# Opening of a state-space kernel generator: first unit's phase and sines moved into the tables' stage

## The chip, the core and the metric

One core of one Trainium2 chip runs the whole program in one launch. The metric is the device time of the program in microseconds (us), the median of three timed runs. The profiles are of single executions of the same program, taken by the hardware profiler.

## What is computed

The reference runs four layers on a sequence of 2048 rows and 640 channels: a state-space convolution, an attention with one shared key and value head, and both again. Only the convolution kernel `K` matters for this change. It is the same for both convolution layers and is generated once, at the start of the program:

```python
dt = jnp.exp(log_dt)[:, None]
logdA = dt * (A_re + 1j * A_im)
P = jnp.exp(logdA[:, :, None] * l[None, None, :])        # 640 x 128 x 2048
K = jnp.einsum("dn,dnl,dn->dl", Cc, P, dt * Bc).real     # 640 x 2048
```

## The kernel before, in words

The program has five parts: the generator of `K` (`kgen`), a convolution, an attention, a convolution and an attention. The change touches the generator, which runs from the start of the program to about 300 us.

The generator has two stages. The first, `kg_tables` (from line 203), is here called **the tables' stage**. On tiles of 128 x 640 it works out four quantities per channel and state: the turn of one step (`thr`), of 32 steps (`th1`), the starting phase (`ph`) and the decay (`are`), with a logarithmic weight (`lw`). Each is split into three bf16 parts in a staging tile `hth1`, `hthr`, `hph`, `hlw`, `hare`. The parts then have to change their layout from channels on partitions to (part, channel) rows, in the three tables `tb` (from `th1`), `ta` (from `thr` and `ph`) and `tm` (from `are` and `lw`). `send` does that through DRAM for `th1`, `thr` and `are`: one copy out (`hd...`) and three back. `send_late` does it straight from the staging tile for `ph` and `lw`: three small copies (one per part, 16 partitions, 20 KB) for each of eight groups q of channels. The 48 small copies are here called **the late sends**; in the order of SyncE they stand as triples, `ta` of group 0, `tm` of group 0, `ta` of group 1, and so on to `tm` of group 7. A copy reads `hph` or `hlw` when it runs, so these two staging tiles are in use until the last late send has landed.

The second stage is the loop over 20 **units** u, each 32 channels by 128 states. A unit goes through these steps:

- `phase(u, h)`, h = 0 or 1: two matmuls (tile `ph`, one buffer in PSUM) give a phase, and VectorE takes its fraction with two instructions, `r` and `f` (128 x 1024).
- `trig(u, h)` on ScalarE: `fa` (absolute value), a sine and a cosine, into `C1`, `S1` for h = 0 and into `C2`, `S2` for h = 1.
- `sizes(u, k)`, k = 0, 1, 2: two matmuls each (tile `pe`, two buffers). k = 0, 1 read the 48 rows of `tm` from `are`; k = 2 reads also the rows from `lw`.
- `exps(u, k)` on ScalarE: exponentials into `M1` (k = 0, 1) and `M2` (k = 2).
- `products(u, k)`: two VectorE instructions each. k = 0 makes `e1r` from `M1` and `C1`, k = 1 multiplies `M1` by `S1`, k = 2 multiplies `C2` and `S2` by `M2`.
- `sums(u, ...)`: 64 small fp32 matmuls into `pk`; `store(u - 3)` copies `pk` to `kst` on ScalarE and, every fourth unit, to DRAM (`kd`).

Sine and exponential use different function tables on ScalarE, so a pair of units is done together: six exponentials, a table load, four `trig`, a table load. Group q of `ta` and `tm` is what unit u = q reads (modulo 8).

The order of PE, ScalarE and VectorE in the loop is written out by hand (`manual_schedule`); the order of SyncE's copies is manual only in the tables' stage, and elsewhere set by the scheduler. Products of unit u - 1, sums of unit u - 2 and phases of unit u + 1 are woven into turn u. `load_x` reads the residual stream `x` (eight copies of 640 KB), which the statistics (`stats`, one call in each of turns 5 to 12, the rest at the end) read.

Tiles come from pools, one region of memory each. All tiles of the tables' stage are in pool `kgq`, which is closed at its end; the loop's pool `kgb` is then opened where `kgq` was. A loop's tile that lies where a tile of the tables' stage lay waits until the earlier tile has been read for the last time.

Of the kernel before, what the change touches and what calls it, by code (L numbers as in the profile page):

```python
# [11 lines left out]
F32 = mybir.dt.float32  # L12
# [9 lines left out]
P = 128  # L22
# [134 lines left out]
class Net:  # L157
# [42 lines left out]
        with ExitStack() as ctx:  # L200
            self._kgen(ctx)

    def kg_tables(self, pp, hs, t3, SH, ldt, aim, are_raw, bre, bim, cre, cim, ta, tb, tm):

        nc = self.nc
        V, S, T, A = (nc.vector.tensor_tensor, nc.vector.scalar_tensor_tensor, nc.vector.tensor_scalar,
                      nc.scalar.activation)
        dt, th, are, thr, th1, ph = pp.tile([P, 5], F32, name="dt"), *(  # L210
            t3(n) for n in ("th", "are", "thr", "th1", "ph"))
        wr, wi, u0, u1, u2, u3, lw = (t3(n) for n in ("wr", "wi", "u0", "u1", "u2", "u3", "lw"))
        ar, ai, mx, mn, gt = (t3(n) for n in ("ar", "ai", "mx", "mn", "gt"))
        res = {n: t3("res" + n) for n in hs}

        def cast(n, src, k):
            A(hs[n][:, k], src if k == 0 else res[n], AF.Copy)

        def rest(n, src, k):
            V(res[n], src if k == 0 else res[n], hs[n][:, k], ALU.subtract)  # L220

        def send(n, dst, between=lambda: None):
            hd = self.dr.tile([P, 3, 5 * NST], BF16, name="hd" + n)
            nc.sync.dma_start(hd, hs[n].rearrange("p k t s -> p k (t s)"))
            between()
# [24 lines left out]
        rest("th1", th1, 0)  # L250
        cast("th1", th1, 1)
        V(mx, ar, ai, ALU.max)
        V(mn, ar, ai, ALU.min)
        T(mx, mx, 1e-37, None, ALU.max)
        rest("th1", th1, 1)
        cast("th1", th1, 2)
        send("th1", tb)
        cast("thr", thr, 0)
        nc.vector.reciprocal(u0, mx)
        V(u0, mn, u0, ALU.mult)  # L260
        for t in range(5):
            A(are[:, t], are_raw[:, t], AF.Copy, scale=dt[:, t : t + 1])
        cast("are", are, 0)

        A(u1, u0, AF.Arctan)
        V(gt, ai, ar, ALU.is_gt)
        rest("thr", thr, 0)
        cast("thr", thr, 1)
        T(wr, wr, 0.0, 0.5, ALU.is_lt, ALU.mult)
        S(u1, gt, 0.5 * math.pi, u1, op0=ALU.mult, op1=ALU.subtract)  # L270
        A(u1, u1, AF.Abs, scale=1.0 / TWO_PI)
        T(wi, wi, 0.0, -2.0, ALU.is_lt, ALU.mult)
        rest("thr", thr, 1)
        V(u1, wr, u1, ALU.subtract)
        A(u1, u1, AF.Abs)
        cast("thr", thr, 2)
        send("thr", ta)
        T(ph, th1, 32.0, None, ALU.mult)
        self.frac(pp, ph, ph, SH)
        S(u1, wi, 1.0, u1, op0=ALU.add, op1=ALU.mult)  # L280
        V(ph, ph, u1, ALU.add)
        self.frac(pp, ph, ph, SH)

        A(u2, u0, AF.Square)
        A(lw, mx, AF.Ln)
        A(u3, u2, AF.Ln, bias=1.0)
        nc.vector.tensor_copy(hs["ph"][:, 0], ph)
        rest("ph", ph, 0)
        nc.vector.tensor_copy(hs["ph"][:, 1], res["ph"])
        rest("ph", ph, 1)  # L290
        nc.vector.tensor_copy(hs["ph"][:, 2], res["ph"])
        rest("are", are, 0)
        cast("are", are, 1)
        S(lw, u3, 0.5, lw, op0=ALU.mult, op1=ALU.add)
        for t in range(5):
            T(lw[:, t], lw[:, t], ldt[:, t : t + 1], None, ALU.add)
        rest("are", are, 1)
        cast("are", are, 2)
        send("are", tm, lambda: send_late(0, ta, hs["ph"]))
        nc.vector.tensor_copy(hs["lw"][:, 0], lw)  # L300
        rest("lw", lw, 0)
        nc.vector.tensor_copy(hs["lw"][:, 1], res["lw"])
        rest("lw", lw, 1)
        nc.vector.tensor_copy(hs["lw"][:, 2], res["lw"])
        for q in range(8):
            if q > 0:
                send_late(q, ta, hs["ph"])
            send_late(q, tm, hs["lw"])

    def _kgen(self, ctx):  # L310
# [11 lines left out]
        with tc.tile_pool(name="kgq", bufs=1) as pp:  # L322
            SH = [P, 5, NST]

            def t3(name):
                return pp.tile(SH, F32, name=name)


            hs = {n: pp.tile([P, 3, 5, NST], BF16, name="h" + n)
                  for n in ("ph", "lw", "th1", "thr", "are")}  # L330
            ldt = pp.tile([P, 5], F32, name="ldt")
            nc.sync.dma_start(ldt, ins["A_log_dt"])
            raw = {}
            for n, eng in (("A_A_im", nc.sync), ("A_C_re", nc.scalar), ("A_B_re", nc.sync),
                           ("A_C_im", nc.scalar), ("A_B_im", nc.sync), ("A_A_re", nc.scalar)):
                raw[n] = t3("r" + n)
                eng.dma_start(raw[n], ins[n].rearrange("(t p) n -> p t n", p=P))
            nc.sync.dma_start(kg, ins["c_kg"])
            bre, bim, cre, cim = (raw["A_" + n] for n in ("B_re", "B_im", "C_re", "C_im"))
            with tc.manual_schedule(engines={mybir.EngineType.Activation, mybir.EngineType.DVE,  # L340
                                             mybir.EngineType.SP}):
                self.kg_tables(pp, hs, t3, SH, ldt, raw["A_A_im"], raw["A_A_re"], bre, bim, cre, cim,
                               ta, tb, tm)

        bp = ctx.enter_context(tc.tile_pool(name="kgb", bufs=2, reuse_waits="tile"))
# [5 lines left out]
        KST[0, 0] = bp.tile([P, 64, 32], F32, tag="kst", bufs=2, name="kst00")  # L351

        def big(tag, u, x, bufs=2):
            return bp.tile([P, 16, 2, x], F32, tag=tag, bufs=bufs, name=f"{tag}_{u}")

        def swap(a):
            return a.rearrange("p d a s -> p a d s")
# [16 lines left out]
        def phase(u, h):  # L374
            if (u, h) not in PH:
                phase_first(u, h)
            pp = PH.pop((u, h))
            r = bp.tile([P, 1024], BF16, tag="r", bufs=2, name=f"r{u}{h}")
            self.magic_round(r, pp)
            F[u, h] = bp.tile([P, 1024], F32, tag="f", bufs=4, name=f"f{u}{h}")  # L380
            nc.vector.tensor_tensor(F[u, h], pp, r, ALU.subtract)

        def trig(u, h):
# [9 lines left out]
            fa = bp.tile([P, 1024], F32, tag="fa", bufs=1, name=f"fa{u}{h}")  # L393
            nc.scalar.activation(fa, f, AF.Abs)
            nc.scalar.activation(s, f.rearrange("p (a d s) -> p a d s", a=2, d=16), AF.Sin, scale=TWO_PI)
            nc.scalar.activation(c, fa.rearrange("p (a d s) -> p a d s", a=2, d=16), AF.Sin,
                                 scale=-TWO_PI, bias=self.halfpi)

        def sizes(u, k):

            pe = PE_[u, k] = kp.tile([P, 1024], F32, tag="pe", bufs=2, name=f"pe{u}{k}")
# [60 lines left out]


        n = len(units)
        engines = {mybir.EngineType.PE, mybir.EngineType.Activation, mybir.EngineType.DVE}
        with tc.manual_schedule(engines=engines):
            for h in range(2):
                phase(0, h)
            for u in range(n + 3):
                now, nxt, prod, tot = u < n, u + 1 < n, 0 < u <= n, 2 <= u < n + 2  # L470
                odd = u % 2 == 1
                if u >= 3:
# [43 lines left out]
                        exps(u, 2)  # L516
                if tot:
                    sums(u - 2, range(7, 8))
                if u == 0:
                    self.load_x()  # L520
                    nc.sync.dma_start(self.ident, ins["c_id"])
                if 5 <= u < 13:
                    self.stats(u - 5)
# [836 lines left out]
```

## Time and profile before

| | |
|---|---|
| median of 3 runs | 3025.67 us (3024.11 to 3025.82) |
| the profiled execution | 3025.52 us, span in the profile 3023.7 us |
| busy, whole span | PE 93%, ScalarE (ACT) 80%, VectorE (DVE) 46%, GpSimd (POOL) 1% |
| tables' stage | 0 to about 43 us |
| opening of the loop (units 0 and 1) | about 43 to 72 us |
| loop over the other units | about 72 to 296 us |
| mean granted clock of TensorE | 0.958 |

Engines in the rows: PE and PEld (TensorE's matmuls and weight loads), DVE, ACT, POOL, and SPq and POOLq for the copies that SyncE and GpSimd issue. L with a number is the line of the kernel before. A timeline row gives start, duration, engine, line, operation, output<-input, sizes and count; in brackets stands the idle time of the engine just before the row, and what ended it. Rows of copies on SPq show the time of issuing, not of the transfer. Clock and DMA columns of a stretch are means over it.

### The profile page before, as it was taken

To read this page: it belongs to the slowest core of one execution; us is meant where nothing else is said; L and a number is where in the kernel's file an instruction comes from. 1 tells how busy PE (TensorE), PEld (TensorE's weight loads), DVE (VectorE), ACT (ScalarE), POOL (GpSimd) and SP (SyncE) were. 2 spreads that over 40 slices of the span, in tenths; PEclk is the share of its full clock that TensorE was granted. 3 is DMA by queue.
4 is the path that set the end of the run, shared out by engine and by line. 5 is a ranking of instruction groups with operands and counts; after the bars stand their busy time and mean duration, and the time that the engine had idled before them with its cause. 6 is when DMAs were issued, how large, how long until landed. Compare 5 with 4: busy or idle time off the path is not lost. (4 is left out here: it accounts for less than half of the span.)

```text
span 3023.7 us, 52365 instructions
## 1 busy us (share of the span) xinstructions
PE 2797.2 (93%) x21696; PEld 1284.0 (42%) x21696; DVE 1402.3 (46%) x1788; ACT 2427.3 (80%) x2910; POOL 45.1 (1%) x117
## 2 busy tenths in 40 slices
PE   2776989998999999999999899798999999999998
PEld 0333979775233323333232689673233333323333
DVE  7999899942123232322323499721222223222222
ACT  5888333444999999999999532438999999999997
POOL 0001000000000000000000000000000000000000
PEclk9855999999999999999999999899999999999999
DMA  6114531133200010000100211131100101110100
GB/s 145 33 22 112 186 143 56 46 115 111 80 22 25 22 27 21 26 25 22 25 22 20 113 56 42 58 131 56 27 24 23 43 22 26 39 28 21 43 19 23
DMA packets 109104, 158.82 MB, mean 53 GB/s; under 512 B 58948, under 2 KB 65092, under 8 KB 105236
## 3 DMA queue, kind: packets, MB, share of 16 engines
q1 hardware_dynamic: 102680, 137.70, 15.7%
q0 software_dynamic: 4208, 16.67, 1.5%
q8 instruction: 175, 2.87, 0.4%
q10 hardware_dynamic: 1968, 0.98, 0.1%
q14 instruction: 73, 0.60, 0.1%
HBM read 95.22 MB, written 48.04 MB: 47 GB/s over the span
## 5 line engine op out<-in xcount | busy, mean ns | idle before, releaser
L1158 ACT ACTIVATE pt<-scb 128x1024 f32<-128x1024 f32 x1024 | 942.2, 1116 | 7.5 <-DMA qpb<-mxd 4.5
L1158 ACT ACTIVATE pt<-scd 128x1024 f32<-128x1024 f32 x1024 | 942.2, 1117 | 7.0 <-PE scd L1154 5.4
L1168 PE MATMUL pod<-pt,vt 128*32 128x512 f32 x4096 | 547.1, 606 | 4.4 <-DVE on L1185 0.2
L1168 PE MATMUL pob<-pt,vt 128*32 128x512 f32 x4096 | 547.0, 606 | 4.4 <-DVE on L1185 0.3
L1154 PE MATMUL scb<-qpb,kt 62*128 62x512 f32 x2048 | 385.9, 451 | 6.2 <-DVEq L1103 5.8
L1154 PE MATMUL scd<-qpd,kt 62*128 62x512 f32 x2048 | 385.9, 451 | 5.6 <-PEq L1103 5.3
L1154 PEld LDWEIGHTS scb<-qpb,kt 62*128 62x128 f32 x2048 | 165.9, 185 | 402.1 <-ACT pt L1158 392.6
L1154 PEld LDWEIGHTS scd<-qpd,kt 62*128 62x128 f32 x2048 | 166.0, 185 | 401.7 <-ACT pt L1158 392.4
L1216 DVE TENSOR_TENSOR x<-pyd,x 128x320 f32<-128x320 f32 x146 | 71.8, 492 | 560.8 <-PE pyd L1228 560.8
L1216 DVE TENSOR_TENSOR x<-pyb,x 128x320 f32<-128x320 f32 x146 | 71.8, 492 | 547.6 <-PE pyb L1228 547.6
L1188 DVE RECIPROCAL rc<-rc 128x512 f32<-128x512 f32 x62 | 207.9, 3354 | 2.1
L1168 PEld LDWEIGHTS pob<-pt,vt 128*32 128x32 f32 x4096 | 80.6, 108 | 178.2 <-issue 160.2
L1168 PEld LDWEIGHTS pod<-pt,vt 128*32 128x32 f32 x4096 | 80.6, 108 | 178.0 <-issue 160.0
L601 PE MATMUL za<-xna,wf 128*128 128x256 f32 x512 | 113.0, 383 | 2.5 <-ACT xna L757 2.5
L601 PE MATMUL zc<-xnc,wf 128*128 128x256 f32 x512 | 111.5, 379 | 2.7 <-ACT xnc L757 2.7
L603 ACT ACTIVATE Aa<-za 128x1024 f32<-128x1024 f32 x16 | 16.4, 1023 | 118.5 <-PE za L601 117.3
L603 ACT ACTIVATE Ac<-zc 128x1024 f32<-128x1024 f32 x16 | 16.4, 1023 | 113.7 <-PE zc L601 113.7
L1228 PE MATMUL pyd<-wo,ot 128*32 128x320 f32 x1168 | 105.3, 432 | 0.0
L1228 PE MATMUL pyb<-wo,ot 128*32 128x320 f32 x1168 | 105.3, 432 | 0.0
L601 PEld LDWEIGHTS za<-xna,wf 128*128 128x128 f32 x512 | 97.8, 192 | 16.6 <-ACT xna L757 3.3
L601 PEld LDWEIGHTS zc<-xnc,wf 128*128 128x128 f32 x512 | 96.9, 190 | 16.3 <-ACT xnc L757 3.3
L800 PE MATMUL yc<-Ac,wi 128*128 128x128 f32 x640 | 78.4, 286 | 15.8 <-DVE Ac L114 13.1
(312 smaller groups left out, 3107.2 us busy)
## 6 DMA issues: line engine op xcount, KB each, us to landing
kh<-kh SPq DMA_DIRECT2D x10, 2048.0 KB
kh<-kn SPq DMA_DIRECT2D x5, 2048.0 KB
qhd<-qh SPq DMA_DIRECT2D x40, 256.0 KB
qld<-ql SPq DMA_DIRECT2D x40, 256.0 KB
qpb<-qhd SPq DMA_DIRECT2D x256, 40.0 KB
qpd<-qhd SPq DMA_DIRECT2D x256, 40.0 KB
ot<-on SPq DMA_DIRECT2D x216, 40.0 KB
wf<-in_c_wf POOLq DMA_DIRECT2D x16, 512.0 KB, 7.9
```

The source lines that it names most:

```text
L601: nc.tensor.matmul(zv[:, :, c, kk], self.wf[:, t + 4 * h, j, c, kk], x, start=(n == 0), stop=(n == 3))
L603: nc.scalar.activation(A.rearrange("p (o s) d -> p o s d", o=2)[:, :, 2 * t : 2 * t + 2], z.rearrange("p (c o e) -> p o c e", c=2, o=2), A ...
L800: nc.tensor.matmul(y[:, s * DC : (s + 1) * DC], self.wi[:, t, j, c_, kk], v[:, 2 * t + c_, kk], start=(i == 0 and not whole), stop=(i == 3 ...
L1154: nc.tensor.matmul(sc[:, 512 * par : 512 * par + 512], kt[rows, 128 * t : 128 * t + 128], qps[nb, hg, pr][rows], start=True, stop=True)
L1158: nc.scalar.activation(pt, sc, AF.Exp, scale=SCALE)
L1168: nc.tensor.matmul(po[32 * j : 32 * j + 32], vt[:, t], pts[step, j // 2][:, 512 * (j % 2) : 512 * (j % 2) + 512], start=(t == 0), stop=(t ...
L1188: nc.vector.reciprocal(rc, rc)
L1216: nc.vector.tensor_tensor(xh, py, xh, ALU.add)
L1228: nc.tensor.matmul(py[j : j + m], o[:, 128 * i + j : 128 * i + j + m], w[:, 320 * half : 320 * half + 320], start=start, stop=stop)
```

## The change

The change does these things:

- `phase(0, 0)` and `trig(0, 0)` of unit 0 are done inside the tables' stage (`begin()`), after the `ph` parts and before `lw` is finished.
- The splitting of `are` and its `send` come earlier, behind those of `thr`; the first triple of late sends (`ta`, group 0) follows it.
- Steps of units 0 and 1 are written out one by one: exponentials of both units first, then the sines `trig(0, 1)`, `trig(1, 0)`, `trig(1, 1)`. Turns from unit 2 on are as before.
- Most tiles of `phase` and `trig` and the `kst` tiles get a pool of their own (`kga`), opened before `kgq`, so that they don't lie where the tables' tiles lie.
- Twelve of the tables' fp32 tiles, the inputs' among them, are put into the memory of `x`. `x` is therefore loaded later: all eight copies stand behind the last late send, and wait for a small ScalarE instruction that writes `x`.
- In `kgq` the staging tiles come first, in the order `are`, `thr`, `th1`, a filler of 768 bytes, `ph`, `lw`.
- The order of SyncE's copies is manual in the loop too, and the load of `ident` stands in every turn from u = 2 to 21 (20 times 64 KB) in place of once.

```diff
-        res = {n: t3("res" + n) for n in hs}
+        res = {n: t3("res" + n) for n in ("ph", "lw", "th1", "thr", "are")}
...
         rest("thr", thr, 0)
         cast("thr", thr, 1)
+        rest("are", are, 0)
+        cast("are", are, 1)
...
         send("thr", ta)
+        rest("are", are, 1)
+        cast("are", are, 2)
+        send("are", tm)
...
         nc.vector.tensor_copy(hs["ph"][:, 2], res["ph"])
-        rest("are", are, 0)
-        cast("are", are, 1)
+        send_late(0, ta, hs["ph"])
+        begin()
         S(lw, u3, 0.5, lw, op0=ALU.mult, op1=ALU.add)
...
-        rest("are", are, 1)
-        cast("are", are, 2)
-        send("are", tm, lambda: send_late(0, ta, hs["ph"]))
...
+        ba = ctx.enter_context(tc.tile_pool(name="kga", bufs=2, reuse_waits="tile"))
...
+            pool = ba if tag in ("c1", "s1") else bp
+            return pool.tile([P, 16, 2, x], F32, tag=tag, bufs=bufs, name=f"{tag}_{u}")
...
+        def begin():
+            phase(0, 0)
+            trig(0, 0)
+
...
+            homes = [self.x.rearrange("p t d -> p (t d)")[:, 640 * k : 640 * k + 640].rearrange(
+                "p (t s) -> p t s", t=5) for k in range(12)]
+            homes += [pp.tile(SH, F32, name=f"t{k}") for k in range(16)]
+
             def t3(name):
-                return pp.tile(SH, F32, name=name)
-
-
-            hs = {n: pp.tile([P, 3, 5, NST], BF16, name="h" + n)
-                  for n in ("ph", "lw", "th1", "thr", "are")}
+                return homes.pop(0)
+
+            hs = {}
+            for n in ("are", "thr", "th1", "", "ph", "lw"):
+                if n:
+                    hs[n] = pp.tile([P, 3, 5, NST], BF16, name="h" + n)
+                else:
+                    pp.tile([P, 192], F32, name="space")
...
-            for h in range(2):
-                phase(0, h)
-            for u in range(n + 3):
+            phase(0, 1)
+            phase_first(1, 0)
+            for k in range(2):
+                sizes(0, k)
+                exps(0, k)
+            phase(1, 0)
+            sizes(0, 2)
+            exps(0, 2)
+            nc.scalar.activation(self.x[:, :, 0], M1[0][:, :, 0, 0], AF.Copy)
+            self.load_x()
+            products(0, 0)
+            for k in range(2):
+                sizes(1, k)
+                exps(1, k)
+            phase(1, 1)
+            sizes(1, 2)
+            exps(1, 2)
+            trig(0, 1)
+            phase(2, 0)
+            products(0, 1)
+            trig(1, 0)
+            phase(2, 1)
+            products(0, 2)
+            trig(1, 1)
+            for u in range(2, n + 3):
...
                 if tot:
                     sums(u - 2, range(7, 8))
-                if u == 0:
-                    self.load_x()
                     nc.sync.dma_start(self.ident, ins["c_id"])
```

How the change moves instructions, at the three places that count. In these rows no time is told; `hph`, `hlw`, `hare` are staging tiles, `m` is `M1` or `M2`, `c`, `s` are `C1`, `C2`, `S1`, `S2`, and a number in a name is a buffer's.

VectorE, end of the tables' stage and start of the loop, before:

```order
L291 CAST hph<-resph 128x640
L220 TENSOR_TENSOR resare<-are,hare 128x640
L294 SCALAR_TENSOR_TENSOR lw<-u_116,lw 128x640
L296 TENSOR_SCALAR lw<-lw,ldt 128x128 x5
L220 TENSOR_TENSOR resare<-resare,hare 128x640
L300 CAST hlw<-lw 128x640
...
L304 CAST hlw<-reslw 128x640
L191 TENSOR_SCALAR r_284<-ph_281 128x1024
L381 TENSOR_TENSOR f_286<-ph_281,r_284 128x1024
```

And now:

```order
L295 CAST hph<-t_98 128x640
L191 TENSOR_SCALAR r_213<-ph_210 128x1024
L358 TENSOR_TENSOR f_215<-ph_210,r_213 128x1024
L298 SCALAR_TENSOR_TENSOR t_92<-t_91,t_92 128x640
L300 TENSOR_SCALAR t_92<-t_92,ldt 128x128 x5
L301 CAST hlw<-t_92 128x640
...
L305 CAST hlw<-t_99 128x640
L191 TENSOR_SCALAR r_291<-ph_288 128x1024
L358 TENSOR_TENSOR f_293<-ph_288,r_291 128x1024
```

The first `r` and `f` of the loop have moved ahead of the `lw` chain (`t_92` is `lw`), and the two `resare` instructions have left this place for one before the `ph` parts.

ScalarE, units 0 and 1, before, with the semaphores that each row waits for:

```order
L396 ACTIVATE c_0_295<-fa_299,halfpi 128x2x16x32 [waits Activation_49]
L394 ACTIVATE fa_318<-f_293 128x1024 [waits DVE_49,Activation_49]
L395 ACTIVATE s_0_317<-f_293 128x2x16x32
L396 ACTIVATE c_0_316<-fa_318,halfpi 128x2x16x32 [waits Activation_49]
L412 ACT_TABLE_LOAD
L412 ACTIVATE m_0_329<-pe_303 128x16x64 [waits PE_49]
...
L394 ACTIVATE fa_391<-f_327 128x1024 [waits DVE_49,Activation_49]
L395 ACTIVATE s_1_390<-f_327 128x2x16x32
L396 ACTIVATE c_1_389<-fa_391,halfpi 128x2x16x32 [waits Activation_49]
L394 ACTIVATE fa_399<-f_364 128x1024 [waits DVE_49,Activation_49]
```

And now:

```order
L373 ACTIVATE c_0_217<-fa_221,halfpi 128x2x16x32 [waits Activation_49]
L424 ACT_TABLE_LOAD
L424 ACTIVATE m_0_301<-pe_298 128x16x64 [waits PE_49]
...
L372 ACTIVATE s_0_350<-f_293 128x2x16x32
L373 ACTIVATE c_0_349<-fa_351,halfpi 128x2x16x32 [waits DMAHW1_49,Activation_49]
...
L371 ACTIVATE fa_383<-f_343 128x1024 [waits DVE_49,Activation_49]
L372 ACTIVATE s_1_382<-f_343 128x2x16x32
L373 ACTIVATE c_1_381<-fa_383,halfpi 128x2x16x32 [waits DMAHW4_49,DMAHW3_49,DMAHW5_49,DMAHW2_49,DMAHW6_49,DMAHW1_49,DMAHW7_49,DMAHW0_49,Activation_49]
L371 ACTIVATE fa_391<-f_360 128x1024 [waits DVE_49,Activation_49]
```

The sines of unit 0's second phase have moved behind the exponentials of both units. The cosine of `trig(1, 1)` (`c_1_381`, the tile `C2` of unit 1), which waited for ScalarE alone, now waits for all eight semaphores of the copies; in the built program its counts are those of the `tm` copies of the late sends up to group 7, whose source `hlw` lay where `C2` of unit 1 now lies.

SyncE's copies around the late sends, before:

```order
L224 DMA hdthr<-hthr 128x1920
L615 DMA x<-in_A_u 64x2560
L227 DMA ta<-hdthr 16x8x640 x3
L224 DMA hdare<-hare 128x1920
L232 DMA ta<-hph 16x640 x3
L615 DMA x<-in_A_u 64x2560
L227 DMA tm<-hdare 16x8x640 x3
L232 DMA tm<-hlw 16x640 x3
L232 DMA ta<-hph 16x640 x3
```

And now:

```order
L224 DMA hdthr<-hthr 128x1920
L226 DMA ta<-hdthr 16x8x640 x3
L224 DMA hdare<-hare 128x1920
L226 DMA tm<-hdare 16x8x640 x3
L231 DMA ta<-hph 16x640 x3
L231 DMA tm<-hlw 16x640 x3
L231 DMA ta<-hph 16x640 x3
...
L648 DMA x<-in_A_u 64x2560 x8
```

The copies of `x` are gone from between the sends; all eight stand behind the sixteenth triple. The triples' own order is the same.

## Rows read from the trace of the kernel before

**Rows 1.** Busy time by stretch: us, PE, PEld, DVE, ACT, POOL, PEclk, DMA share, GB/s

```profile
0.00:20.00 20.00, 0.00 (x0) 0.00 (x0) 13.25 (x23) 5.37 (x8) 0.20 (x4) 1.00 0.94 237
20.00:44.00 24.00, 1.03 (x2) 0.13 (x2) 23.14 (x35) 12.23 (x19) 0.34 (x4) 1.00 0.79 174
44.00:60.00 16.00, 6.15 (x14) 1.40 (x14) 7.99 (x8) 11.36 (x11) 0.00 (x0) 1.00 0.57 93
...
200.00:250.00 50.00, 37.24 (x578) 17.11 (x582) 49.55 (x46) 43.70 (x45) 2.03 (x9) 0.53 0.17 22
```

**Rows 2.** Timeline of ACT, the loop from unit 1's second cosine

```profile
71.40 1.13 ACT L396 ACTIVATE c<-fa,halfpi 128x1024 f32<-128x1024 f32 x1
...
80.03 1.94 ACT L412 ACTIVATE m<-pe 128x1024 f32<-128x1024 f32 x2
...
86.53 1.02 ACT L412 ACTIVATE m<-pe 128x1024 f32<-128x1024 f32 x1 [1.80 <-PE pe L404]
...
104.40 1.94 ACT L412 ACTIVATE m<-pe 128x1024 f32<-128x1024 f32 x2
...
184.46 1.02 ACT L412 ACTIVATE m<-pe 128x1024 f32<-128x1024 f32 x1 [2.27 <-PE pe L404]
...
209.78 1.02 ACT L412 ACTIVATE m<-pe 128x1024 f32<-128x1024 f32 x1 [2.75 <-PE pe L404]
...
276.38 1.94 ACT L412 ACTIVATE m<-pe 128x1024 f32<-128x1024 f32 x2
```

**Rows 3.** Timeline of DVE, first product of units 2, 4, 6 and 18

```profile
84.28 1.22 DVE L422 TENSOR_TENSOR e1r<-m,c 128x1024 f32<-128x1024 f32 x1
...
107.54 1.22 DVE L422 TENSOR_TENSOR e1r<-m,c 128x1024 f32<-128x1024 f32 x1
...
132.87 1.21 DVE L422 TENSOR_TENSOR e1r<-m,c 128x1024 f32<-128x1024 f32 x1
...
279.00 1.23 DVE L422 TENSOR_TENSOR e1r<-m,c 128x1024 f32<-128x1024 f32 x1 [0.35 <-PE pk L441]
```

**Rows 4.** Timeline behind the loop: GpSimd's weight copies and the first spectrum's matmuls

```profile
283.84 4.23 POOL L554 DMA_DIRECT2D wf<-in_c_wf  x8 [9.64 <-PE pe L404]
...
300.63 8.64 PE L572 MATMUL zk<-Rk,wf 128*128 128x128 f32 x61 [1.17 <-DMA Rk<-kd]
```

**Rows 5.** Timeline of DVE, end of the tables' stage and opening

```profile
42.51 0.49 DVE L304 CAST hlw<-reslw 128x640 bf16<-128x640 f32 x1
...
54.95 1.22 DVE L191 TENSOR_SCALAR r<-ph 128x1024 bf16<-128x1024 f32 x1 [5.49 <-PE ph L371]
...
72.62 1.22 DVE L422 TENSOR_TENSOR e1r<-m,c 128x1024 f32<-128x1024 f32 x1
```

**Rows 6.** Timeline of SyncE's copies around the late sends

```profile
29.86 0.34 SPq L224 DMA_DIRECT2D hdthr<-hthr  x1
...
40.62 0.34 SPq L224 DMA_DIRECT2D hdare<-hare  x1
...
43.65 1.48 SPq L227 DMA_DIRECT2D tm<-hdare  x3
45.17 1.78 SPq L232 DMA_DIRECT2D tm<-hlw  x3
47.00 4.54 SPq L232 DMA_DIRECT2D ta<-hph  x3
52.23 1.84 SPq L232 DMA_DIRECT2D tm<-hlw  x3
...
75.31 2.35 SPq L232 DMA_DIRECT2D tm<-hlw  x3
```

**Rows 7.** Waits of SyncE's queue in the first 110 us: total us, times, longest

```profile
SPq L232 <- DMA x<-in_A_u: 2.2, 1, 2.2
...
SPq L232 <- DMA tm<-hdare: 1.5, 3, 0.7
```

**Rows 8.** DMA issues: KB, median us from issue to landing

```profile
ktl<-in_A_Dskip POOLq DMA_DIRECT2D x1, 0.5 KB, 2.0
```

More of the change, by code (lines that the diff above doesn't have):

```diff
@@ L201, in kgen, with kg_tables @@
             self._kgen(ctx)
-    def kg_tables(self, pp, hs, t3, SH, ldt, aim, are_raw, bre, bim, cre, cim, ta, tb, tm):
+    def kg_tables(self, pp, hs, t3, SH, ldt, aim, are_raw, bre, bim, cre, cim, ta, tb, tm, begin):
         nc = self.nc
@@ L220, in rest, with send @@
             V(res[n], src if k == 0 else res[n], hs[n][:, k], ALU.subtract)
-        def send(n, dst, between=lambda: None):
+        def send(n, dst):
             hd = self.dr.tile([P, 3, 5 * NST], BF16, name="hd" + n)
             nc.sync.dma_start(hd, hs[n].rearrange("p k t s -> p k (t s)"))
-            between()
             for k in range(3):
@@ L320, in _kgen @@
         kg = sp.tile([96, 2560], BF16, name="kg")
-        with tc.tile_pool(name="kgq", bufs=1) as pp:
-            SH = [P, 5, NST]
-            def t3(name):
-                return pp.tile(SH, F32, name=name)
-            hs = {n: pp.tile([P, 3, 5, NST], BF16, name="h" + n)
-                  for n in ("ph", "lw", "th1", "thr", "are")}
[L331 to L345, printed above, removed]
+        ba = ctx.enter_context(tc.tile_pool(name="kga", bufs=2, reuse_waits="tile"))
         units = [(q, r, q * 256 + 16 * r, 128, 128) for q in range(2) for r in range(8)]
@@ L350, in _kgen @@
         C1, S1, C2, S2, M1, M2, E1R, F, PH, PE_, PK, KST = ({} for _ in range(12))
-        KST[0, 0] = bp.tile([P, 64, 32], F32, tag="kst", bufs=2, name="kst00")
+        KST[0, 0] = ba.tile([P, 64, 32], F32, tag="kst", bufs=2, name="kst00")
         def big(tag, u, x, bufs=2):
-            return bp.tile([P, 16, 2, x], F32, tag=tag, bufs=bufs, name=f"{tag}_{u}")
+            pool = ba if tag in ("c1", "s1") else bp
+            return pool.tile([P, 16, 2, x], F32, tag=tag, bufs=bufs, name=f"{tag}_{u}")
         def swap(a):
@@ L377, in phase @@
             pp = PH.pop((u, h))
-            r = bp.tile([P, 1024], BF16, tag="r", bufs=2, name=f"r{u}{h}")
+            r = ba.tile([P, 1024], BF16, tag="r", bufs=2, name=f"r{u}{h}")
             self.magic_round(r, pp)
-            F[u, h] = bp.tile([P, 1024], F32, tag="f", bufs=4, name=f"f{u}{h}")
+            F[u, h] = ba.tile([P, 1024], F32, tag="f", bufs=4, name=f"f{u}{h}")
             nc.vector.tensor_tensor(F[u, h], pp, r, ALU.subtract)
@@ L392, in trig @@
             f = F.pop((u, h))
-            fa = bp.tile([P, 1024], F32, tag="fa", bufs=1, name=f"fa{u}{h}")
+            fa = ba.tile([P, 1024], F32, tag="fa", bufs=1, name=f"fa{u}{h}")
             nc.scalar.activation(fa, f, AF.Abs)
@@ L397, in trig, with t3 @@
                                  scale=-TWO_PI, bias=self.halfpi)
+        def begin():
+            phase(0, 0)
+            trig(0, 0)
+        with tc.tile_pool(name="kgq", bufs=1) as pp:
+            SH = [P, 5, NST]
+            homes = [self.x.rearrange("p t d -> p (t d)")[:, 640 * k : 640 * k + 640].rearrange(
+                "p (t s) -> p t s", t=5) for k in range(12)]
+            homes += [pp.tile(SH, F32, name=f"t{k}") for k in range(16)]
+            def t3(name):
+                return homes.pop(0)
[5 more added lines that the diff above has]
+                    pp.tile([P, 192], F32, name="space")
+            ldt = pp.tile([P, 5], F32, name="ldt")
+            nc.sync.dma_start(ldt, ins["A_log_dt"])
+            raw = {}
+            for n, eng in (("A_A_im", nc.sync), ("A_C_re", nc.scalar), ("A_B_re", nc.sync),
+                           ("A_C_im", nc.scalar), ("A_B_im", nc.sync), ("A_A_re", nc.scalar)):
+                raw[n] = t3("r" + n)
+                eng.dma_start(raw[n], ins[n].rearrange("(t p) n -> p t n", p=P))
+            nc.sync.dma_start(kg, ins["c_kg"])
+            bre, bim, cre, cim = (raw["A_" + n] for n in ("B_re", "B_im", "C_re", "C_im"))
+            with tc.manual_schedule(engines={mybir.EngineType.Activation, mybir.EngineType.DVE,
+                                             mybir.EngineType.SP, mybir.EngineType.PE}):
+                self.kg_tables(pp, hs, t3, SH, ldt, raw["A_A_im"], raw["A_A_re"], bre, bim, cre, cim,
+                               ta, tb, tm, begin)
+        bp = ctx.enter_context(tc.tile_pool(name="kgb", bufs=2, reuse_waits="tile"))
         def sizes(u, k):
@@ L447, in store @@
             if g == 0 and u > 0:
-                KST[q, h] = bp.tile([P, 64, 32], F32, tag="kst", bufs=2, name=f"kst{q}{h}")
+                KST[q, h] = ba.tile([P, 64, 32], F32, tag="kst", bufs=2, name=f"kst{q}{h}")
             kst = KST[q, h]
@@ L464, in _kgen @@
         n = len(units)
[L465 removed]
+        engines = {mybir.EngineType.PE, mybir.EngineType.Activation, mybir.EngineType.DVE,
+                   mybir.EngineType.SP}
         with tc.manual_schedule(engines=engines):
[L467 to L469 removed]
+            phase(0, 1)
[23 more added lines that the diff above has]
+            for u in range(2, n + 3):
                 now, nxt, prod, tot = u < n, u + 1 < n, 0 < u <= n, 2 <= u < n + 2
```

## The prediction

> **What bounds the kernel now.** I looked at the busy time by stretch first, because the change touches only the first 72 us. At the end of the tables' stage VectorE is full (23.14 of 24 us), in the opening it is busy 7.99 of 16 us, and later in the loop again 49.55 of 50 [rows 1]. So the opening holds about 8 us of idle time on VectorE, and the change reorders just that. The reader should then ask whether VectorE really sets the pace of the loop, since only then are those 8 us worth 8.
>
> The ScalarE timeline says it doesn't. The exponentials of the even units start at 80.03 and 104.40, so a pair of units takes 24.37 us. The last such start is 276.38, eight pairs after the first [rows 2]; eight times 24.37 is 194.96, and the distance is 196.35. VectorE's first product of a unit starts at 84.28 and 107.54, a pair of 23.26 us; with two calls of the statistics it is 25.33 (107.54 to 132.87) [rows 3]. Yet the pair on ScalarE stays 24.37 while VectorE's differs by 2 us from pair to pair. So the loop's pace is that of the cycle through ScalarE and PE: sizes wait for a free `pe` buffer, exponentials for sizes, with a wait of 1.80 us that recurs in each pair [rows 2]. VectorE trails it by a slack: 84.28 - 80.03 = 4.25 us at unit 2, 3.14 at unit 4, and 2.62 at unit 18, where it does wait (0.35 us for the sums that read the buffer) [rows 2, 3]. The eight calls of the statistics add about 1 us a turn to that slack; at the height of it the cycle is held up, by 0.47 and 0.95 us (the 1.80 grown to 2.27 and 2.75) [rows 2]. These 1.42 us are the whole difference between 196.35 and 194.96.
>
> What follows the loop hangs on the same cycle. The weight copies wait for the last sizes on PE, at 283.84, and the first matmul of the spectra waits for copies in the same stream [rows 4]. A loop that ends later moves all that follows by as much.
>
> **So the question is one number: when does unit 1's last cosine run?** In the kernel before, the cosine of `trig(1, 1)` starts at 71.40; behind it ScalarE does the two `trig` of unit 2 and a table load without a pause and begins unit 2's exponentials at 80.03, 8.63 us later [rows 2]. From that cosine on, ScalarE's order is the same in both kernels. If it moves by d, the loop moves by d, less what the slack gives back.
>
> **The change, part by part.**
>
> *Tables' stage.* The `are` splits go ahead of the `ph` parts; the same instructions, no more in sum than before. Of unit 0's first phase, `r` and `f` go ahead of the `lw` chain: two instructions of 1.22 us [rows 5], 2.5 us with the dependence between them. `hlw` was ready at 43.0 (42.51 + 0.49) [rows 5]; it will be at 45.5. On ScalarE `trig(0, 0)` now fills time that was idle, at no cost.
>
> *Opening, as far as compute goes.* VectorE no longer stands 5.49 us before the third `r` [rows 5]. `f` of (0, 1) should end between 47.9 and 49.7: `r` can start at 45.5 when `hlw` is done, or when the first triple of `ta` has landed, which I put at up to 47. That is worked out so: `hthr` goes out at 29.86 before, about 0.9 us later now (one step stands ahead of its last part), so 30.8; from a copy out to the copies back 3.0 us (40.62 to 43.65), 1.5 us for these, the same again for `hare`, and 1.8 for the triple [rows 6], which makes 41.6; and 5.4 us to land, since the three copies `tm<-hdare`, issued by 45.13, held SyncE until some time before 52.23 in the same traffic [rows 6, 7]. Exponentials of (0, 0) start 2.1 us behind `f`, for (1, 0)'s phase and the first sizes stand between them on PE. From there to the cosine in question I count 16.6 us: 7.1 for six exponentials with their waits for sizes, 4.5 for a table load and the three instructions of `trig(0, 1)`, 3.1 for `trig(1, 0)`, and 1.9 for the two ahead of the cosine (each about 1 us, a load 1.28; the same kinds from cosine to exponentials took the 8.63 above). Compute would let that cosine start at 66.6 to 68.4, which is 3 to 4.8 us earlier than 71.40.
>
> *The new wait.* But this cosine now waits for the last late send, since its output lies where `hlw` lay. So the sum is made on SyncE's queue. SyncE issues the third copy of `tm`, group 0, once `hlw` is ready, at 45.6, and is through at 46.2. 14 triples follow. From the triple at 52.23 to the end of the last one (75.31 + 2.35 = 77.66) it took 25.43 us for 13 triples, 1.96 each [rows 6]. 14 times 1.96 is 27.4, so the last is issued at 73.6, its third copy begun at about 72.9. Landing is not in the rows of SyncE's queue. Its bounds: below, nothing after issue (73.6); above, 4.5 us after it, as a copy's semaphore is used again by the eighth copy after it, and no wait for that is seen at the steady pace (78.1). The nearest row is the small copy on GpSimd's queue, 2.0 us from issue to landing [rows 8]; with it the send lands at 74.9, and the cosine starts at 75.1.
>
> The Trainium skill, "DMA: Bandwidth & Descriptors", section "Anatomy of one DMA — SWDGE (gpsimd) path", gives a copy a fixed 2.0 us, most of it the receipt after the last byte. By it, counted from the end of issue, the landing would be at 75.6 and the sum 0.7 us larger (an estimate from that page). No row here times a copy on SyncE's queue to its landing.
>
> *Sum.* 75.1 - 71.40 = 3.7 us later. The slack gives some back: unit 2's first product waits on PE's sums behind the exponentials, so VectorE trails by the least, 2.62, and at unit 4 by 2.62 in place of 3.14. With 0.52 us less at the start of the statistics the two hold-ups shrink from 1.42 to about 0.9. Net 3.7 - 0.5 = **3.2 us slower**.
>
> *Edits that I cost at nothing.* `x` is loaded at 74 to about 100; 5.2 MB at some 230 GB/s (the program's first 20 us moved 237 [rows 1]) is 23 us, and its first reader, the first call of the statistics, stands in turn 5, some 15 us past the exponentials of unit 4 at 104.40 [rows 2]. If that cover is gone, VectorE waits there. The loads of `ident` take 64 KB each, on a queue that is idle between the `kst` stores. The number of table loads is the same.
>
> **The rivals.**
>
> (a) *The wait is over before the cosine needs it.* The late sends land by 68, say because SyncE issues faster when `x` doesn't stand between them. Then the cosine moves by -3.9 us (67.5), and VectorE, whose order gains only 2 to 3.7 us (its first product of unit 1 at about 69 to 70.7 in place of 72.62 [rows 5]), trails by 1.1 more and costs that at the statistics: 2.8 us faster, 3022.7. For it: all idle time of the opening. Against: the pace of 1.96 us was the same with no copy of `x` between the triples [rows 6].
>
> (b) *Slower by more than what can be told.* Before, the triple at 47.00 took 4.54 us and the next began at 52.23, 3.3 us more than a triple, because SyncE may not run more than eight copies ahead and waited for `x` (2.2) and for the copies of `tm` from DRAM (1.5) [rows 6, 7]. `x` is gone, but `hare` now goes out right behind the three `ta` copies, in the same traffic. They are issued by 39.8 (30.8 and twice 4.5), so I expect them landed by 46, with up to 6 us as above. If they land up to 3.3 us later, the stall recurs, every send is 3.3 us later, and so is the cosine: 3.2 + 3.3 = 6.5 us slower, 3032.0. It decides once they land after 46.2, where SyncE needs their semaphores.
>
> (c) *VectorE sets the loop's pace after all.* Then only its own lateness counts: its first product of unit 2 can start at 75.1 + 8.63 + 2.62 = 86.35 against 84.28 [rows 3], 2.1 us slower, 3027.6. For it: 99% busy [rows 1]. Against: the constant 24.37.
>
> **How the numbers follow.** The profiled execution took 3025.52 us, 0.15 under the median of the runs. The forecast is 3025.5 + 3.2 = **3028.7 us**, with 0.66; by the bounds of the landing its own range is 3027.4 to 3031.9. Rival (a) 0.16, (b) 0.10, (c) 0.08. A measurement of this kernel can tell about 0.2%, 6.05 us, from no change; so the forecast, (a) and (c) all count as the same, and (b) as slower. I put 0.04 on faster, for what a shift of the opening may do to TensorE's clock behind it, and 0.10 on slower. The range of 3022.0 to 3032.0 takes in (a), (c), the forecast's own range to 3031.9 and with it (b); outside it lie an (a) that gains more and a (b) that costs more, and what the clock may do.
>
> **What would show it.** In the changed profile: an idle time of ScalarE of 6 to 9 us before the cosine of `trig(1, 1)`, ended by a copy `tm<-hlw`, and its start near 75; the exponentials of unit 2 at 83.7; pairs still 24.37 us apart; the opening's stretch on VectorE fuller but an idle time of about 5 us before unit 2's first product. I am wrong if that cosine starts before 71, if ScalarE doesn't stand before it, or if the time behind 310 us changes by itself.

## The result, and the profile after

| | before | after |
|---|---|---|
| median of 14 runs each (lowest to highest) | 3024.40 us (3022.94 to 3026.79) | 3030.76 us (3027.47 to 3033.76) |
| ratio | | 1.0021 [1.0013, 1.0030], so 3.9 to 9.1 us slower |
| profiled execution | 3025.52 us | 3033.76 us (the highest of the 14) |
| cosine of `trig(1, 1)` starts | 71.40 | 76.88 |
| exponentials of unit 2 / unit 20 start | 80.03 / 276.38 | 85.54 / 281.88 |

The change is slower, by a hair more than the 0.2% that the prediction set as its bound. ScalarE in the changed kernel, rows as in [rows 2]; the brackets give the idle time just before a row and what ended it:

```profile
52.68 1.94 ACT L424 ACTIVATE m<-pe 128x1024 f32<-128x1024 f32 x2 [5.79 <-PE pe L416]
...
68.24 1.04 ACT L372 ACTIVATE s<-f 128x1024 f32<-128x1024 f32 x1
76.88 1.15 ACT L373 ACTIVATE c<-fa,halfpi 128x1024 f32<-128x1024 f32 x1 [7.60 <-DMA tm<-hlw]
...
85.54 1.94 ACT L424 ACTIVATE m<-pe 128x1024 f32<-128x1024 f32 x2
...
109.92 1.94 ACT L424 ACTIVATE m<-pe 128x1024 f32<-128x1024 f32 x2
...
189.92 1.02 ACT L424 ACTIVATE m<-pe 128x1024 f32<-128x1024 f32 x1 [2.14 <-PE pe L416]
...
215.22 1.02 ACT L424 ACTIVATE m<-pe 128x1024 f32<-128x1024 f32 x1 [2.72 <-PE pe L416]
...
281.88 1.94 ACT L424 ACTIVATE m<-pe 128x1024 f32<-128x1024 f32 x2
```

The idle time of 7.60 us, ended by a copy `tm<-hlw`, is the new wait. (A line with three dots stands for rows left out.) ScalarE was ready for this cosine at 76.88 - 7.60 = 69.28, which is 2.1 us earlier than it ran before; but it ran 5.48 us later (76.88 against 71.40). Unit 2 is 5.51 us later, unit 20 is 5.50 later: the loop passes the delay on whole. SyncE's copies, rows as in [rows 6]:

```profile
42.15 1.83 SPq L231 DMA_DIRECT2D ta<-hph  x3
44.07 2.65 SPq L231 DMA_DIRECT2D tm<-hlw  x3
46.77 1.84 SPq L231 DMA_DIRECT2D ta<-hph  x3
...
71.44 1.84 SPq L231 DMA_DIRECT2D tm<-hlw  x3
73.39 5.92 SPq L648 DMA_DIRECT2D x<-in_A_u  x8
```

The stall of [rows 6] at 47.00 (4.54 us) is gone. The last triple is issued by 71.44 + 1.84 = 73.28, and the cosine starts 3.6 us later. The trace also has the moments at which the 16 parts of a copy land: 15 parts of the last copy had landed at 74.52 and the sixteenth at 76.25. The section on `x` behind the wait comes back to that. VectorE, rows as in [rows 3] and [rows 5]:

```profile
48.22 1.22 DVE L191 TENSOR_SCALAR r<-ph 128x1024 bf16<-128x1024 f32 x1 [2.03 <-PE ph L348]
...
70.90 1.22 DVE L434 TENSOR_TENSOR e1r<-m,c 128x1024 f32<-128x1024 f32 x1
...
88.16 1.23 DVE L434 TENSOR_TENSOR e1r<-m,c 128x1024 f32<-128x1024 f32 x1 [5.52 <-PE pk L453]
...
112.54 1.23 DVE L434 TENSOR_TENSOR e1r<-m,c 128x1024 f32<-128x1024 f32 x1 [0.57 <-PE pk L453]
...
119.95 1.23 DVE L191 TENSOR_SCALAR r<-ph 128x1024 bf16<-128x1024 f32 x1 [0.38 <-PE ph L348]
```

VectorE did gain in the opening: its first product of unit 1 starts at 70.90 in place of 72.62. Then it stands 5.52 us, because unit 2 comes late on ScalarE. So the change moved the idle time from ahead of unit 1 to ahead of unit 2.

Behind the generator this execution loses some more. The first projections of the first attention start at 625.72 in the kernel before and at 631.35 in the changed one, 5.63 us later, as the generator left them. The busy time by stretch from there, columns as in [rows 1], in the kernel before:

```profile
625.70:630.00 4.30, 4.28 (x19) 2.61 (x20) 1.69 (x2) 4.07 (x7) 0.00 (x0) 1.00 0.00 0
```

and in the changed one, two stretches:

```profile
631.30:635.60 4.30, 4.25 (x10) 2.08 (x11) 1.73 (x2) 3.54 (x5) 0.00 (x0) 0.50 0.00 0
635.60:640.00 4.40, 4.40 (x20) 3.30 (x19) 0.68 (x1) 1.67 (x3) 0.00 (x0) 0.98 0.05 13
```

The granted clock is 0.50 (the lower of TensorE's two levels) for 4.3 us, in which it does 10 matmuls where it did 19. ScalarE then waits longer for the first projection; before:

```profile
629.43 0.59 ACT L1037 ACTIVATE qh<-pqb 52x512 fp32r<-52x512 f32 x1 [0.23 <-PE pqb L1025]
```

and in the changed kernel:

```profile
637.08 0.59 ACT L1070 ACTIVATE qh<-pqb 52x512 fp32r<-52x512 f32 x1 [2.24 <-PE pqb L1058]
```

That is 2.0 us on top of the generator's 5.5, in this execution.

### The profile page after: what moved, and what is told of

It is laid out like the page before. It is cut to its first block, busy times and chain, and to the rows that moved or that the text cites. A ratio compares the mean times of both kernels' runs of the same rounds, so it can differ in the third digit from the quotient of the medians.

```text
span 3031.9 us, 52412 instructions
## 1 busy us (share of the span) xinstructions
PE 2797.3 (92%) x21696; PEld 1283.6 (42%) x21696; DVE 1402.2 (46%) x1788; ACT 2430.4 (80%) x2911; POOL 45.1 (1%) x117
## 3 DMA queue, kind: packets, MB, share of 16 engines
q8 instruction: 175, 2.87, 0.4%
```

## The experiments

The theory was that one wait, that of `trig(1, 1)`'s cosine for the last late send, makes the time. Rivals: VectorE sets the pace and the wait is hidden; the late `x` or the repeated `ident` cost the time. The changed kernel's time is that of the result (14 runs). Every other kernel was timed in five rounds against the kernel before, 11 runs each (6 of the wait put into before). A summary first; "wait" is ScalarE's idle time before that cosine.

| kernel | wait | cosine | unit 2 | unit 20 | median | ratio to before |
|---|---|---|---|---|---|---|
| before | 0 | 71.40 | 80.03 | 276.38 | | |
| after | 7.60 | 76.88 | 85.54 | 281.88 | 3030.76 | 1.0021 [1.0013, 1.0030] |
| staging elsewhere | 0 | 69.42 | 78.04 | 274.87 | 3024.35 | 1.0000 [0.9991, 1.0009] |
| wait put into before | 8.20 | 79.37 | 88.01 | 284.29 | 3033.42 | 1.0032 [1.0020, 1.0044] |
| sends on two queues | 0 | 69.62 | 78.25 | 275.08 | 3024.60 | 1.0001 [0.9992, 1.0010] |
| `ident` once | 7.36 | 76.57 | 85.21 | 281.52 | 3030.96 | 1.0020 [1.0011, 1.0029] |
| `x` behind the wait | 7.35 | 76.62 | 85.27 | 281.54 | 3030.99 | 1.0020 [1.0011, 1.0029] |
| exponentials first | 0 | 64.87 | 73.48 | 272.16 | 3022.47 | 0.9992 [0.9983, 1.0001] |
| first send earlier | 0 | 64.67 | 73.30 | 271.97 | 3021.61 | 0.9993 [0.9984, 1.0002] |
| phase first on PE | 0 | 64.46 | 73.08 | 271.17 | 3019.96 | 0.9986 [0.9977, 0.9995] |

**The wait taken out of the change.** Only the places of tiles in `kgq` differ: `hph` and `hlw` lie under the third buffer of `M1`, which is first written by the exponentials of unit 2. (The list of the change says that the staging tiles come first in `kgq`. In the kernel they stand behind the sixteen fp32 tiles `t0` to `t15`, which is how the last two of them come to lie under `C2`.)

```diff
-            homes += [pp.tile(SH, F32, name=f"t{k}") for k in range(16)]
+            homes += [pp.tile(SH, F32, name=f"t{k}") for k in range(3)]
+            pp.tile([P, 128], F32, name="space")
+            hs = {n: pp.tile([P, 3, 5, NST], BF16, name="h" + n) for n in ("ph", "lw")}
+            homes += [pp.tile(SH, F32, name=f"t{k}") for k in range(3, 16)]
+            hs.update({n: pp.tile([P, 3, 5, NST], BF16, name="h" + n) for n in ("are", "thr", "th1")})
...
```

> The change, with hph and hlw placed under the third buffer of M1 instead of under C2 of units 2 and 1. Theory (the wait of the cosine of trig(1,1) for the last late send makes the time): in the change ScalarE stood 7.60 us before that cosine, so it now starts at 69.3; the exponentials of unit 2, which now write where the staging lay, start at 77.9, 1 us after the last send has landed (76.9), so they hardly wait. The loop starts 2.1 us earlier than before, VectorE's first product of unit 1 1.7 us earlier; the time is 1.5 to 2 us under before (about 3022.5) and about 8 us under the change. Rival (VectorE sets the loop, or the late x and the 20 loads of ident cost the time): the cosine starts earlier, but the time stays within 2 us of the change, near 3030.

ScalarE in that kernel:

```profile
69.42 1.13 ACT L373 ACTIVATE c<-fa,halfpi 128x1024 f32<-128x1024 f32 x1
...
78.04 1.94 ACT L422 ACTIVATE m<-pe 128x1024 f32<-128x1024 f32 x2
...
84.80 1.02 ACT L422 ACTIVATE m<-pe 128x1024 f32<-128x1024 f32 x1 [2.07 <-PE pe L414]
...
274.87 1.94 ACT L422 ACTIVATE m<-pe 128x1024 f32<-128x1024 f32 x2
```

No idle time before the cosine, unit 2 at 78.04 as expected, and the whole loss is gone: 3024.35 against 3030.76. The gain of 1.5 to 2 us beside before that was expected is there in the generator (276.38 - 274.87 = 1.5) and not to be seen in the median (0.5 us, with an interval of 2.7 either way). This profile too has ScalarE wait 2.3 us for the first projections.

**The wait put into the kernel before.** Again only places differ:

```diff
-        ar, ai, mx, mn, gt = (t3(n) for n in ("ar", "ai", "mx", "mn", "gt"))
+        ar = t3("ar")
+        pp.tile([P, 496], F32, name="space")
+        hs.update({n: pp.tile([P, 3, 5, NST], BF16, name="h" + n) for n in ("ph", "lw")})
+        ai, mx, mn, gt = (t3(n) for n in ("ai", "mx", "mn", "gt"))
...
-                  for n in ("ph", "lw", "th1", "thr", "are")}
+                  for n in ("th1", "thr", "are")}
```

> The kernel before, with hph and hlw placed under C2 of units 2 and 1, nothing else. Theory: the wait alone slows the kernel. SyncE ended the issue of the sends at 77.66 in before, and in the change the last one landed 3.6 us behind the end of issue (73.28 to 76.88); so here it lands at about 81.2, the cosine of trig(1,1) is 9.8 us later than 71.40, the exponentials of unit 2 start at about 89.9, and the time is 9 to 10 us over before, about 3034. Rival (what the loop loses at its start it makes up from slack): within 3 us of before.

SyncE's last late sends in that kernel:

```profile
72.75 2.18 SPq L235 DMA_DIRECT2D ta<-hph  x3
74.98 2.87 SPq L235 DMA_DIRECT2D tm<-hlw  x3
77.90 0.59 SPq L618 DMA_DIRECT2D x<-in_A_u  x1
```

and ScalarE:

```profile
79.37 1.15 ACT L399 ACTIVATE c<-fa,halfpi 128x1024 f32<-128x1024 f32 x1 [8.20 <-DMA tm<-hlw]
...
88.01 1.94 ACT L415 ACTIVATE m<-pe 128x1024 f32<-128x1024 f32 x2
```

With the old opening, the early `x` and one load of `ident`, the wait alone makes the kernel 0.32% slower. Unit 2 is 88.01 - 80.03 = 7.98 us later, not 9.8, because here the cosine starts 1.5 us behind the end of issue (74.98 + 2.87 = 77.85) and not 3.6. The median is 8.6 us over before, where 9 to 10 were expected.

**The copies made faster.**

```diff
-                nc.sync.dma_start(dst[48 + 16 * k : 64 + 16 * k, q].rearrange("d t s -> d (t s)"),
+                (nc.gpsimd if dst is tm else nc.sync).dma_start(dst[48 + 16 * k : 64 + 16 * k, q].rearrange("d t s -> d (t s)"),
```

> The change, with the 24 copies tm<-hlw issued by GpSimd; SyncE keeps the 24 ta<-hph. Theory: each queue has half the copies, at 0.6 us each about 15 us, so all have landed by about 65; the cosine of trig(1,1) starts at 69.3 without a wait and the time is that of the kernel with the staging elsewhere, about 3022.5. Rival (something else in the opening, not these copies, sets the time): the wait is gone, the time stays near 3030.

GpSimd in that kernel:

```profile
44.07 11.64 POOL L231 DMA_DIRECT2D tm<-hlw  x24 [43.00 <-DVE hlw L301]
```

All 24 copies are out by 55.7, and by the table of DMA issues (KB each, median us to landing)

```profile
tm<-hlw POOLq DMA_DIRECT2D x24, 20.0 KB, 2.1
```

they land 2.1 us after their issue began. The wait is gone without any tile being moved, and the time is that of the kernel with the staging elsewhere. Two ways to lift the same wait give the same time; with the wait added to before, that settles the cause.

**The two other suspects.** `ident` loaded once:

```diff
+                if u == 2:
                     nc.sync.dma_start(self.ident, ins["c_id"])
```

> The change, with ident loaded once (u = 2) in place of 20 times. Theory: no effect, the cosine still waits until 76.9 and the time is within 1 us of the change, about 3030.5. Rival (the repeated loads or their traffic cost part of the 6.4 us that were measured): 1 to 3 us under the change.

Nothing: 3030.96, the wait is 7.36. The 19 further loads cost no time that can be seen, as the prediction said. `x` loaded behind the wait:

```diff
-            nc.scalar.activation(self.x[:, :, 0], M1[0][:, :, 0, 0], AF.Copy)
-            self.load_x()
...
             trig(1, 1)
+            nc.scalar.activation(self.x[:, :, 0], M1[0][:, :, 0, 0], AF.Copy)
+            self.load_x()
```

> The change, with the loads of x (and the small ScalarE instruction that they wait for) behind trig(1,1), so that no x moves while the last sends land. Theory A (the traffic of x stretches the landing of the last send: 3.6 and 3.2 us behind the end of issue with eight copies of x right behind it, 1.5 us in the kernel before with the wait, where one copy of x stood behind): the cosine of trig(1,1) starts 1.5 to 2 us behind the end of issue, at about 75.0 in place of 76.9, and the time is about 1.8 us under the change. Theory B (these copies land 3.5 us behind their issue whatever follows): still 76.9, the time as the change.

SyncE, then ScalarE in that kernel:

```profile
71.59 1.84 SPq L231 DMA_DIRECT2D tm<-hlw  x3
77.92 5.51 SPq L648 DMA_DIRECT2D x<-in_A_u  x8
```

```profile
76.62 1.15 ACT L373 ACTIVATE c<-fa,halfpi 128x1024 f32<-128x1024 f32 x1 [7.35 <-DMA tm<-hlw]
```

My theory A fell. No `x` moves before 77.92, yet the cosine starts 76.62 - 73.43 = 3.2 us behind the end of issue, as it does with `ident` once, where `x` follows at once. So the traffic of `x` isn't what stretches the landing. Theory B, 3.5 us whatever follows, doesn't fit the 1.5 us of the wait put into before either. The traces hold a third answer: the landing of each of a copy's 16 parts, and the packets of the queue that the profile calls `instruction`.

| kernel | last copy, end of issue | its 15th part landed | its 16th part landed | 16 KB packet of instructions | cosine starts |
|---|---|---|---|---|---|
| after | 73.28 | 74.52 | 76.25 | 73.88 to 75.07 | 76.88 |
| `ident` once | 73.37 | 74.61 | 75.94 | 73.83 to 74.86 | 76.57 |
| `x` behind the wait | 73.43 | 74.68 | 76.29 | 73.88 to 75.21 | 76.62 |
| wait put into before | 77.86 | 79.11 | 79.14 | 75.37 to 76.84 | 79.37 |

Fifteen parts land 1.25 us behind the end of issue in all four. In the first three the sixteenth is 1.3 to 1.7 us later, and its data packet starts (75.06, 74.86, 75.19) within 0.02 us of the end of the packet of instructions. With the wait put into before, that packet comes ahead of the last copy and meets two copies before it (their last parts land at 77.92 and 78.10, where the other fifteen had landed by 76.17 and 76.86). By these times a load of instructions held up one part of the copy that the cosine waits for. That the two shared a DMA engine is inferred from these times, for the trace doesn't name the engine of a packet, and no kernel here was built to move that load.

**What the opening can give.** With the wait gone, VectorE's idle time is what is left. On top of the sends on two queues, units 0 and 1 in another order:

```diff
-            phase(0, 1)
-            phase_first(1, 0)
             for k in range(2):
                 sizes(0, k)
                 exps(0, k)
-            phase(1, 0)
+            phase(0, 1)
+            products(0, 0)
+            for k in range(2):
+                sizes(1, k)
+                exps(1, k)
             sizes(0, 2)
+            phase(1, 0)
             exps(0, 2)
...
```

> The kernel with the sends on two queues, and the steps of units 0 and 1 in another order: sizes and exponentials of (0,0), (0,1) ahead of the phase (0,1), then (1,0), (1,1), (0,2), (1,2); one or two product instructions between each two phases. Theory (behind the wait, VectorE's own idle time in the opening is what is left to gain: 1.13 + 0.41 + 0.81 + 1.13 = 3.5 us before the third product in the change, and ScalarE's 5.8 us before the first exponential): the exponentials of (0,0) start at about 47, unit 2's at about 73.5, VectorE's first product of unit 2 at about 79.3 against 83.0 with the sends on two queues; VectorE then trails by more and the loop gives part back at the statistics; the loop ends 3 to 4 us earlier than there and the time is 4 to 5.5 us under before, about 3020. Rival (the loop's pace allows no more): 1 to 2 us under before, as there.

VectorE in that kernel:

```profile
49.43 1.23 DVE L191 TENSOR_SCALAR r<-ph 128x1024 bf16<-128x1024 f32 x1 [3.18 <-PE ph L348]
...
80.10 1.22 DVE L434 TENSOR_TENSOR e1r<-m,c 128x1024 f32<-128x1024 f32 x1
```

and ScalarE:

```profile
73.48 1.94 ACT L424 ACTIVATE m<-pe 128x1024 f32<-128x1024 f32 x2
...
82.10 1.02 ACT L424 ACTIVATE m<-pe 128x1024 f32<-128x1024 f32 x1 [3.17 <-PE pe L416]
...
99.97 1.94 ACT L424 ACTIVATE m<-pe 128x1024 f32<-128x1024 f32 x2
```

ScalarE is 4.8 us ahead at unit 2, but VectorE then trails by 80.10 - 73.48 = 6.6 us and the next sizes come 3.17 us late, so that the pair takes 26.5 us. The loop ends 2.9 us earlier than with the sends on two queues. The median is 2.0 us under before, with an interval that just takes in no change; I had expected 4 to 5.5.

VectorE still stands 3.18 us before `r`. So the first triple goes out while SyncE waits for `hdare`:

```diff
-        send("are", tm)
+        hdare = send("are", tm, between=True)
...
         send_late(0, ta, hs["ph"])
+        back(hdare, tm)
         begin()
```

> The kernel with the exponentials first, and the first triple ta<-hph issued ahead of the three copies tm<-hdare, while SyncE waits for hdare anyway (it stood from 35.6 to 40.6 there, hph is ready at 38.7). Theory (the opening of that kernel is set by VectorE alone: from the second r at 49.43 on it never stands until the loop's last units, and ahead of it it stood 3.18 us for the first triple): the triple lands 3 us earlier, r starts at 46.5 right behind the last part of hlw, the whole of VectorE's order moves by 2.9 us, unit 2's first product to about 77.2, the loop's end by 2.5 to 2.9; the time is 2 to 3 us under the kernel with the exponentials first, about 3020. Rival (the copies tm<-hdare now land later and hold the first exponentials, ScalarE sets the pace): less than 1 us.

A miss: the median is 2.7 us under before, only 0.7 more than that of the exponentials first, where 2 to 3 more were expected, and VectorE's row hardly moved,

```profile
49.24 1.23 DVE L191 TENSOR_SCALAR r<-ph 128x1024 bf16<-128x1024 f32 x1 [2.93 <-PE ph L354]
```

and PE shows why:

```profile
46.37 1.86 PE L422 MATMUL pe<-kg,tm 48*128 48x512 bf16 x4 [16.01 <-DMA tm<-hdare]
48.16 1.04 PE L354 MATMUL ph<-kg,ta 96*128 96x512 bf16 x2
```

The phase's matmuls had their table, but stood behind the sizes in PE's order. "Ended by PE" named the engine, not the cause. With `phase_first(0, 1)` ahead of the sizes:

> The kernel with the first send earlier, and the two matmuls of phase (0,1) ahead of the sizes of unit 0 on PE. There they stood behind the sizes, which wait for tm<-hdare until 46.3, so that r stayed at 49.24 although its triple had gone out at 36.0 to 39.3. Theory (PE's order was all that held r): r starts at 46.4, right behind the last part of hlw, VectorE's order moves by 2.8 us and with it the loop; exponentials of units 4 to 20 start 2.5 to 2.8 us earlier (unit 20 at about 269.3), the time is 2 to 3 us under that kernel, about 3019. Rival (unit 2's exponentials, at 73.3 either way, set the loop): less than 0.5 us.

VectorE in that kernel:

```profile
46.10 1.22 DVE L191 TENSOR_SCALAR r<-ph 128x1024 bf16<-128x1024 f32 x1
49.90 1.23 DVE L440 TENSOR_TENSOR e1r<-m,c 128x1024 f32<-128x1024 f32 x1 [1.32 <-ACT m L430]
53.07 1.22 DVE L191 TENSOR_SCALAR r<-ph 128x1024 bf16<-128x1024 f32 x1 [0.80 <-PE ph L354]
```

`r` starts 3.1 us earlier, but 2.1 us of it are lost to waits for the exponentials and the next phase, and the loop ends 0.8 us earlier (271.17 against 271.97). Half right: PE's order held `r`, but not `r` alone held VectorE. That the median came near the expected 3019 all the same doesn't bear the theory out: the loop gave 0.8 us of the 2.5 to 2.8 expected, and the rest of the step from the kernel ahead of it lies within the two intervals. The kernel is 5.1 us faster than before, 0.9986 [0.9977, 0.9995], against 1.0021 for the change: 0.35% between the two. It keeps the change's begin in the tables' stage and is the best version found.

## Why the prediction was right, and what of it was off

The forecast was 3.2 us slower; measured are 6.4 [3.9, 9.1], within the range, and slower where most of the chance stood on a loss. By the prediction's own bound of 0.2% the median falls on the side that it called slower, to which it had given 0.10; the interval of 0.13 to 0.30% takes in the bound. The step that decides, the new wait, was right in its place, its releaser and its sign, and the two kernels that lift it and the one that adds it show that nothing else in the change costs time beyond the intervals. Point by point:

- *What bounds the loop.* Right. In the changed kernel VectorE trails at unit 2 by 88.16 - 85.54 = 2.62 us, exactly the least slack taken, pairs take 24.38 us, and the delay at unit 2 is the delay at unit 20.
- *The opening's own work.* ScalarE was ready at 69.28, not at 66.6 to 68.4. The 16.6 us from the first exponential to the cosine were right to the hundredth (52.68 + 16.6 = 69.28); but `r` began at 48.22 in place of 45.5 to 47. The first triple had landed at 46.9, the upper end of the estimate, and two matmuls of the phase (1.0 us), which that estimate left out, stand between landing and `r`. It didn't count, since the wait covered it.
- *Issue of the sends.* Forecast by 73.6, measured 73.28.
- *Landing: the mis-sized term.* I took 2.0 us from the beginning of the last copy, the row of GpSimd's queue, so a landing at 74.9 and the cosine at 75.1. The landing was at 76.25 and the cosine at 76.88, inside the bounds given (73.6 to 78.1). This is 1.8 of the 2.3 us by which the loop's delay was underestimated. The row was right for SyncE's copies in their steady stream too: the median of the 48 late sends is 1.8 us from the beginning of issue to landing, and 15 of the last copy's 16 parts had landed at 74.52. What the sum lacked is the delay of the sixteenth part, 1.7 us, beside a load of instructions; also, the cosine started 0.6 us behind the landing where the sum had 0.2. The estimate from the Trainium skill, "DMA: Bandwidth & Descriptors", section "Anatomy of one DMA — SWDGE (gpsimd) path", came nearer with 75.6 only by its number: counted from the end of issue its 2.0 us are more than the 1.25 us that the undisturbed parts took, and counted from the beginning they agree with the 1.8 us.
- *Slack given back: 0.5 us, measured none.* The two hold-ups shrank to 0.34 and 0.92 us from 0.47 and 0.95, which is 0.16. At unit 4 VectorE trails by 2.62 us (112.54 - 109.92), as forecast, but it also waits there for the sums and for `ph` (0.57 us and, at 119.95, 0.38), and by unit 6 it trails by 4.04 where it trailed by 4.11: most of what it was ahead is lost.
- *From 5.5 to 6.4 us.* The rest is within the interval. TensorE's lower level at the first projections (2.0 us in the profiled execution) can make such a difference; it is also the third sign of being wrong that the prediction named, a time behind 310 us that changes by itself. ScalarE's wait for them is 1.5 to 2.3 us in the profiles of the change, of `ident` once, of `x` behind the wait and of the staging elsewhere, and 0.2 to 0.4 us in the six others, before among them. The four profiled executions with the long wait are 0.6 to 3.0 us over the medians of their kernels, the six others between 1.0 under and 1.3 over, which speaks for the executions. One execution of each kernel doesn't settle it, so this stays open.
- *Rival (a)* is what the kernels without the wait do: unit 2 is 2.0 us earlier and the loop's end 1.5, where I had 3.9 and 2.8. *Rival (b)* gave a time close to the measured one for a wrong reason: its stall of 3.3 us, a wait for copies to land, didn't come back. The 0.8 us that the triple at 44.07 took beyond 1.84 are a wait for the last part of `hlw` on VectorE, which the forecast had in its sum. *Rival (c)* would hold for a VectorE that trails more, as with the exponentials first.
- *Costed at nothing.* Right for `ident`. `x` never held VectorE: no idle time of it ends with `x`.

## What to carry to other kernels

A staging tile that is the source of a long row of small copies lives until the last of them has landed; put it under a tile that is first written well after that. Here the place alone, with no instruction moved, was worth 6.4 us in the change (3030.76 to 3024.35) and 8.6 in the kernel before (3024.81 in the same rounds, to 3033.42). Before you fill an engine's idle time, find the engine whose period stays constant when the other's varies: idle time on the other is worth only what the first gains. And where an idle time is put down to PE, look at what stands ahead in PE's own order. Where a wait for a copy is longer than its neighbours', look at the landing of its single parts, and at what else the DMA queues carried then.

## What the runs showed of the hardware

- 24 copies of 20 KB took SyncE 15.2 us to issue and GpSimd 11.6 us, side by side. The landing doesn't set the two queues apart: the last copy of each in that kernel landed 1.2 to 1.3 us behind the end of its issue.
- Of SyncE's late sends in the changed kernel half landed within 1.24 us of the end of issue. The last one took 2.97 us, for its sixteenth part; in three kernels that part's data packet started as a 16 KB packet of instructions, 1.0 to 1.3 us long, ended. A wait for a copy ends with the slowest of its parts.
- The first projections of the attention start at TensorE's lower level in four of the ten profiles (granted clock 0.50, 0.50, 0.50 and 0.67 over their first 4.3 us) and at the higher in six (1.00), behind the same work. ScalarE's wait there differs by up to 2.1 us (0.21 to 2.31), the size of the gain that was looked for.
